# A chunked linear-attention scan with two expert layers: the order of two groups of small matmuls, and 104 rows in a third

## Chip, cores and metric

The kernel runs on one core of a Trainium2 chip. The metric is the device time of one execution in microseconds (us), as the median of several runs. The engines are called PE (TensorE), DVE (VectorE), ACT (ScalarE), POOL (GpSimd) and SP (the queue that issues most DMAs).

## What is computed

Inputs `r, k, v, w, a, b` have the shape (4 batches, 8 heads, 768 steps, 40). Each batch and head carries a 40 x 40 state through the 768 steps:

```python
for t in range(S):
    y[:, :, t] = np.einsum('bhd,bhde->bhe', rt, state)
    Sa = np.einsum('bhde,bhe->bhd', state, at)
    state_decay = state * wt[:, :, None, :] - np.einsum('bhd,bhe->bhde', Sa, bt)
    state = state_decay + np.einsum('bhd,bhe->bhde', vt, kt)
```

The output, 3072 tokens of width 320, then passes through two mixture-of-experts layers (a gate picks one of 8 experts per token; 320 to 1024, relu, back to 320, scaled by the gate's probability; the second layer adds a bias per modality to its gate). The change touches the scan alone.

## The kernel before

The 768 steps are cut into 24 chunks of 32 (`L`), four chunks to a group. Inside a chunk the recurrence is written as matrix products: a triangular system couples its 32 steps, and the state is touched once per chunk. For each chunk the methods of `Chunk` issue, in this order on PE: `x_v` (line 515) and `x_z` (522), the right side of the system from the values and from the state `zs`; `s_t(0)` and `s_t(1)` (562), transposes of the state, which ACT copies to `ssb` (563); between them `y_c` (599) of the chunk before; `r_t` (504), transposes of the next chunk's r; `u_` (533), the product with the solved triangle, whose result U is copied by ACT into `vu` next to v (537); `y_s` (589), the output's part from the state; `z_` (548), the state update; `v_t` (572), transposes of v and U, which ACT copies to `vT` (573); and `c_` (580), the products of r with v and U, masked by DVE (583). Behind `z_`, `z_up` adds the update to the state and applies the decay on DVE (554 and 556); the next chunk's `x_z` and `s_t` read the result.

The layout matters for the change. In `vu` and in the keys, the partitions 0 to 63 and 64 to 127 hold two batches (`u` = 0, 1), each as 32 steps of v (or k) and 32 rows of U (or b); the other two batches lie beside them in the free dimension (`vv` = 0, 1). In the state `zs`, partitions 0 to 63 and 64 to 127 hold heads 0 to 3 and 4 to 7 (`i2` = 0, 1; head h is 4 x `i2` + `p`), of which only the rows 0 to 39 and 64 to 103 are in use, since the head dimension is 40; the other rows are zero. So each matmul of `z_` loads 128 rows by 64 columns of keys, with a stride of 32 elements between columns, and writes to one half of the output partitions, that is, to one column half of PE's array (columns 0 to 63 or 64 to 127). `v_t` transposes 64 rows at a time, which is one row half of the array. `c_` alternates between the column halves `u` = 0 and 1 at each instruction already.

The order of the work is fixed by hand (`tc.manual_schedule`): the loop over `cc` near line 727 calls the steps one after another, and the tables `HOW`, `plan`, `todo` and `extra` put the preparation of later chunks (`aps` line 332, `kps` 345, `aab` 357), the gate of finished chunks (`xt` 1653, `lp` 1661, `rp` 974 to 976) and expert work into numbered slots between them. `Fill` spreads the solves of later triangles and decay products over DVE between the steps (lines 388, 394, 478, 481). `Warm` puts spare matmuls (`wps`, 867) ahead of some PSUM tiles, by the table `PADS`. Each engine works through its own queue in order, and PSUM tiles with the tag `tp` share three buffers.

Of the kernel before, what the change touches and what calls it, by code (L numbers as in the profile page):

```python
# [11 lines left out]
F32 = mybir.dt.float32  # L12
# [4 lines left out]
P = 128  # L17
B, H, S, D = 4, 8, 768, 40
# [36 lines left out]
def attention(tc, zones, ident, r, k, v, w, a, b, emit_x, hook0, hook1, hook2, hook3, unsafe, extra, tail):  # L55
    nc = tc.nc
    with ExitStack() as ctx:
        cp = ctx.enter_context(tc.tile_pool(name="a_const", bufs=1))
        wp = ctx.enter_context(tc.tile_pool(name="a_work", bufs=2))
        ps = Warm(tc, ctx.enter_context(tc.tile_pool(name="a_psum", bufs=1, space=PSUM)), ident)  # L60
# [431 lines left out]
        class Chunk:  # L492
# [46 lines left out]
            def z_(self):  # L539
                kb, c = self.st["kb"], self.c  # L540
                if self.cc + 1 == NCH:
                    return
                self.zps = zps = ps.tile([P, 2, 512], F32, tag="z", name="zps", bufs=1)
                for h in range(H):
                    i2, p = h // 4, h % 4
                    for vv in range(2):
                        o = zps[64 * i2 : 64 * i2 + 64, vv, 0:320].rearrange("q (u p d) -> q u p d", u=2, p=4)[:, :, p]
                        nc.tensor.matmul(out=o, lhsT=kb[:, vv, i2, :, 4 * p + c], rhs=self.vuv[:, vv, :, h, :], start=True, stop=True, skip_group_check=True)  # L548

            def z_up(self, nqlf, nc_):  # L550
                if self.cc + 1 == NCH:
# [6 lines left out]
            def s_t(self, pj):  # L558
                self.ssb = ssb = sst.rearrange("q (p b d) -> q p b d", p=4, b=4)
                sps = ps.tile([P, 4, 2, 64], F32, tag="tp", name="sps", bufs=3)  # L560
                for bb in range(4):
                    nc.tensor.transpose(out=sps[: 2 * D, bb].rearrange("q i e -> q (i e)"), in_=self.zs[:, bb, 2 * pj : 2 * pj + 2].rearrange("q p d -> q (p d)"), identity=ident)
                nc.scalar.copy(ssb[: 2 * D, pj : 4 : 2], sps[: 2 * D, :, :, 0:D].rearrange("q b i e -> q i b e"))

            def v_t(self):
                self.vT = vT = vtt.rearrange("q (u v p x) -> q u v p x", u=2, v=2, p=4)
                for u in range(2):
                    vps = ps.tile([P, 2, 4, 64], F32, tag="tp", name="vps", bufs=3)
                    s0 = slice(64 * u, 64 * u + 64)
                    for vv in range(2):  # L570
                        for hp in range(4):
                            nc.tensor.transpose(out=vps[: 2 * D, vv, hp], in_=self.vuv[s0, vv, u, 2 * hp : 2 * hp + 2].rearrange("q h d -> q (h d)"), identity=ident[s0, s0])
                    nc.scalar.copy(vT[: 2 * D, u], vps[: 2 * D])

            def c_(self):
                cps = ps.tile([P, 2, H, L], F32, tag="tp", name="cps", bufs=3)
# [74 lines left out]
        with tc.manual_schedule():  # L651
# [75 lines left out]
            for cc in range(NCH):  # L727
                g, c = cc // 4, cc % 4
# [1079 lines left out]
```

## Time and profile before

| | us |
|---|---|
| median of 3 runs | 1045.78 |
| lowest and highest | 1043.07, 1052.84 |
| the profiled execution | 1048.63 |
| its span | 1046.4 |
| PE busy in the span | 940.5 (90%) |
| DVE busy in the span | 706.4 (68%) |
| ACT busy in the span | 506.9 (48%) |

The profile is of one execution on the one core; its mean granted PE clock is 0.949 of 2.4 GHz. Each fp32 matmul appears in it as two passes, each a weight load (PEld) and a matmul (PE); a transpose appears as one. Passes overlap: the time of one includes its way through the array, so that starts lie closer together than a pass is long.

### The profile page before, as it was taken

To read this page: it belongs to the slowest core of one execution; us is meant where nothing else is said; L and a number is where in the kernel's file an instruction comes from. 1 tells how busy PE (TensorE), PEld (TensorE's weight loads), DVE (VectorE), ACT (ScalarE), POOL (GpSimd) and SP (SyncE) were. 2 spreads that over 40 slices of the span, in tenths; PEclk is the share of its full clock that TensorE was granted. 3 is DMA by queue.
4 is the path that set the end of the run, shared out by engine and by line. 5 is a ranking of instruction groups with operands and counts; after the bars stand their busy time and mean duration, and the time that the engine had idled before them with its cause. 6 is when DMAs were issued, how large, how long until landed. Compare 5 with 4: busy or idle time off the path is not lost. (4 is left out here: it accounts for less than half of the span.)

```text
span 1046.4 us, 38197 instructions
## 1 busy us (share of the span) xinstructions
PE 940.5 (90%) x16089; PEld 872.4 (83%) x16089; DVE 706.4 (68%) x2022; ACT 506.9 (48%) x991; POOL 298.5 (29%) x361
## 2 busy tenths in 40 slices
PE   7758996888897999988997989999999999999995
PEld 7747875777786888877886989999999999999995
DVE  7799868899798785863443635454556677667662
ACT  6524442443543567654441534444434456656662
POOL 6550020212111111102122425334452533233221
PEclk9769987989999999999998999999999999999998
DMA  5554423342451444234304543544534111172110
GB/s 177 135 136 110 66 82 93 63 117 62 106 125 31 104 105 99 37 52 107 80 15 111 139 130 87 143 126 115 148 88 129 38 47 46 41 233 61 36 43 26
DMA packets 152421, 96.41 MB, mean 92 GB/s; under 512 B 127407, under 2 KB 139585, under 8 KB 151850
## 3 DMA queue, kind: packets, MB, share of 16 engines
q1 hardware_dynamic: 138154, 72.53, 27.6%
q0 software_dynamic: 14080, 21.28, 7.8%
q8 instruction: 130, 2.13, 0.9%
q14 instruction: 57, 0.47, 0.2%
HBM read 112.18 MB, written 14.59 MB: 121 GB/s over the span
## 5 line engine op out<-in xcount | busy, mean ns | idle before, releaser
L1285 PE MATMUL hp<-xs,h 128*128 128x256 f32 (+1 forms) x840 | 156.1, 316 | 0.0
L1296 PE MATMUL yp<-h,hh 128*114 128x320 f32 (+1 forms) x464 | 146.6, 316 | 0.0
L1297 PE MATMUL yp<-l,hh 128*114 128x320 f32 (+1 forms) x464 | 144.1, 311 | 0.0
L1298 PE MATMUL yp<-h,hl 128*114 128x320 f32 (+1 forms) x464 | 143.9, 310 | 0.0
L1288 DVE SCALAR_TENSOR_TENSOR hl<-hp,hh 128x456 fp32r<-128x456 f32 (+1 forms) x116 | 76.6, 661 | 90.4 <-ACT hh L1287 85.2
L1285 PEld LDWEIGHTS hp<-xs,h 128*128 128x128 f32 x840 | 123.6, 189 | 3.3
L1287 ACT ACTIVATE hh<-hp 128x456 fp32r<-128x456 f32 (+1 forms) x116 | 66.5, 574 | 109.9 <-PE hp L1285 92.7
L1285 PE MATMUL hp<-xs,l 128*128 128x256 f32 (+1 forms) x504 | 101.9, 311 | 0.0
L1206 DVE TENSOR_TENSOR l<-s,h 128x768 fp32r<-128x768 f32 x88 | 80.7, 956 | 11.9 <-ACT h L1205 7.5
L1297 PEld LDWEIGHTS yp<-l,hh 128*114 128x114 f32 (+1 forms) x464 | 85.1, 183 | 0.2
L1296 PEld LDWEIGHTS yp<-h,hh 128*114 128x114 f32 (+1 forms) x464 | 85.0, 183 | 0.1
L1298 PEld LDWEIGHTS yp<-h,hl 128*114 128x114 f32 (+1 forms) x464 | 85.0, 183 | 0.0
L1285 PEld LDWEIGHTS hp<-xs,l 128*128 128x128 f32 x504 | 79.4, 188 | 3.1
L1241 POOL DMA_INDIRECT xg<-x,le x52 | 61.6, 1184 | 67.7 <-issue 50.7
L1212 DVE TENSOR_TENSOR l<-s,h 128x640 fp32r<-128x640 f32 x88 | 72.7, 826 | 3.3 <-ACT h L1211 3.3
L1353 POOL DMA_INDIRECT out<-yo,ti x28 | 33.9, 1211 | 129.7 <-ACT yo L1349 76.6
L1205 ACT CAST h<-s 128x768 fp32r<-128x768 f32 x88 | 70.4, 835 | 0.0
L1211 ACT CAST h<-s 128x640 fp32r<-128x640 f32 x88 | 63.3, 719 | 0.0
L388 DVE TENSOR_TENSOR pr<-z_sol 128x110 f32<-128x110 f32 (+20 forms) x232 | 58.1, 280 | 3.9
L977 POOL TENSOR_TENSOR ccnt<-ccnt,oh 128x8 bf16<-128x8 bf16 x24 | 5.1, 211 | 193.7 <-PE rp L975 167.8
L548 PE MATMUL zps<-vu,z_wide 128*64 128x80 f32 x512 | 56.5, 285 | 1.7 <-ACT vu L537 0.7
L995 POOL DMA_INDIRECT lst<-l2e,posi x32 | 40.0, 1250 | 61.6 <-DVE posi L988 54.3
(364 smaller groups left out, 2027.9 us busy)
## 6 DMA issues: line engine op xcount, KB each, us to landing
s<-moe_w SPq DMA_DIRECT2D x22, 1280.0 KB
s<-moe_w SPq DMA_DIRECT2D x22, 1024.0 KB
s<-moe_w SPq DMA_DIRECT2D x44, 256.0 KB
z_w<-w SPq DMA_DIRECT2D x40, 160.0 KB
z_kb<-k SPq DMA_DIRECT2D x24, 160.0 KB
z_kb<-b SPq DMA_DIRECT2D x24, 160.0 KB
z_pa<-a SPq DMA_DIRECT2D x96, 40.0 KB
rt<-r SPq DMA_DIRECT2D x96, 40.0 KB
```

The lines of the kernel that those rows point to most:

```text
L388: nc.vector.tensor_mul(prv, am[:, a:z, s : s + 1].to_broadcast([P, z - a, s + 1]), tm[:, s : s + 1, : s + 1].to_broadcast([P, z - a, s + 1]))
L1205: nc.scalar.copy(wt["h1"][:, :, s], wt["s1"][:, :, s])
L1206: nc.vector.tensor_sub(wt["l1"][:, :, s], wt["s1"][:, :, s], wt["h1"][:, :, s].bitcast(F32))
L1211: nc.scalar.copy(wt["h2"][:, s], wt["s2"][:, s])
L1212: nc.vector.tensor_sub(wt["l2"][:, s], wt["s2"][:, s], wt["h2"][:, s].bitcast(F32))
L1241: d = self.nc.gpsimd.indirect_dma_start(out=b.xg[:, h], out_offset=None, in_=b.lay.src, in_offset=IndirectOffsetOnAxis(ap=b.le[:, h, 0:1]. ...
L1285: nc.tensor.matmul(out=hp[:, i], lhsT=l, rhs=r, start=k == 0, stop=k == len(ops) - 1)
L1287: nc.scalar.activation(hh[:, s], hp, AF.Relu)
L1288: nc.vector.scalar_tensor_tensor(out=hl[:, s], in0=hp, scalar=0.0, in1=hh[:, s].bitcast(F32), op0=ALU.max, op1=ALU.subtract)
L1296: nc.tensor.matmul(out=yp, lhsT=hh[:, k, t], rhs=wt["h2"][:, k], start=k == 0, stop=False)
L1297: nc.tensor.matmul(out=yp, lhsT=hh[:, k, t], rhs=wt["l2"][:, k], start=False, stop=False)
L1298: nc.tensor.matmul(out=yp, lhsT=hl[:, k, t], rhs=wt["h2"][:, k], start=False, stop=k == 7)
```

## The change

In `z_`, the loop over heads (first all of `i2` = 0, then all of `i2` = 1) becomes a loop over `p` and `vv` with `i2` innermost, so that each instruction goes to the other column half than the one before. In `v_t`, the loop over the row halves `u` moves inside, with both `vps` tiles allocated first and the two ACT copies last. In `s_t`, the transposes read the first 104 rows of the state in place of 128, with a 104 x 104 piece of the identity as the moving matrix, and write 104 columns. The number of instructions and every product stay the same.

```diff
@@ z_
-                for h in range(H):
-                    i2, p = h // 4, h % 4
+                for p in range(4):
                     for vv in range(2):
-                        o = zps[64 * i2 : 64 * i2 + 64, vv, 0:320].rearrange("q (u p d) -> q u p d", u=2, p=4)[:, :, p]
-                        nc.tensor.matmul(out=o, lhsT=kb[:, vv, i2, :, 4 * p + c], rhs=self.vuv[:, vv, :, h, :], start=True, stop=True, skip_group_check=True)
+                        for i2 in range(2):
+                            o = zps[64 * i2 : 64 * i2 + 64, vv, 0:320].rearrange("q (u p d) -> q u p d", u=2, p=4)[:, :, p]
+                            nc.tensor.matmul(out=o, lhsT=kb[:, vv, i2, :, 4 * p + c], rhs=self.vuv[:, vv, :, 4 * i2 + p, :], start=True, stop=True, skip_group_check=True)
@@ s_t
+                n = 64 + D
                 for bb in range(4):
-                    nc.tensor.transpose(out=sps[: 2 * D, bb].rearrange("q i e -> q (i e)"), in_=self.zs[:, bb, 2 * pj : 2 * pj + 2].rearrange("q p d -> q (p d)"), identity=ident)
+                    nc.tensor.transpose(out=sps[: 2 * D, bb].rearrange("q i e -> q (i e)")[:, :n], in_=self.zs[:n, bb, 2 * pj : 2 * pj + 2].rearrange("q p d -> q (p d)"), identity=ident[:n, :n])
@@ v_t
+                vps = [ps.tile([P, 2, 4, 64], F32, tag="tp", name="vps", bufs=3) for u in range(2)]
+                for vv in range(2):
+                    for hp in range(4):
+                        for u in range(2):
+                            s0 = slice(64 * u, 64 * u + 64)
+                            nc.tensor.transpose(out=vps[u][: 2 * D, vv, hp], in_=self.vuv[s0, vv, u, 2 * hp : 2 * hp + 2].rearrange("q h d -> q (h d)"), identity=ident[s0, s0])
                 for u in range(2):
-                    vps = ps.tile([P, 2, 4, 64], F32, tag="tp", name="vps", bufs=3)
-                    s0 = slice(64 * u, 64 * u + 64)
-                    for vv in range(2):
-                        for hp in range(4):
-                            nc.tensor.transpose(out=vps[: 2 * D, vv, hp], in_=self.vuv[s0, vv, u, 2 * hp : 2 * hp + 2].rearrange("q h d -> q (h d)"), identity=ident[s0, s0])
-                    nc.scalar.copy(vT[: 2 * D, u], vps[: 2 * D])
+                    nc.scalar.copy(vT[: 2 * D, u], vps[u][: 2 * D])
```

PE's queue in chunk 15, from the last part of `aps` through `z_` and `v_t`, before (`zps` is the output of `z_`, `vps` of `v_t`, each with the number of its buffer; in brackets the queues that an instruction waits for):

```order
L332 MATMUL aps_7700<-ident_75,z_atok_72 128x128 x3
L548 MATMUL zps_7712<-vu1_147,z_wide_70 64x2x40 [waits DMAHW6_49,DMAHW5_49,Activation_49]
L548 MATMUL zps_7712<-vu1_147,z_wide_70 64x2x40 [waits DMAHW7_49,DMAHW0_49,Activation_49]
L548 MATMUL zps_7712<-vu1_147,z_wide_70 64x2x40 x14
L572 MATMUL vps_7732<-ident_75,vu1_147 80x64 [waits PE_49]
L572 MATMUL vps_7732<-ident_75,vu1_147 80x64 x7
L572 MATMUL vps_7742<-ident_75,vu1_147 80x64 [waits PE_49]
L572 MATMUL vps_7742<-ident_75,vu1_147 80x64 x7
```

and the same place after the change (the lines of `v_t` are now 573 and 575):

```order
L332 MATMUL aps_7700<-ident_75,z_atok_72 128x128 x3
L548 MATMUL zps_7712<-vu1_147,z_wide_70 64x2x40 [waits DMAHW6_49,DMAHW5_49,Activation_49]
L548 MATMUL zps_7712<-vu1_147,z_wide_70 64x2x40
L548 MATMUL zps_7712<-vu1_147,z_wide_70 64x2x40 [waits DMAHW7_49,DMAHW0_49,Activation_49]
L548 MATMUL zps_7712<-vu1_147,z_wide_70 64x2x40 x13
L573 MATMUL vps_7732<-ident_75,vu1_147 80x64 [waits PE_49]
L573 MATMUL vps_7733<-ident_75,vu1_147 80x64 [waits PE_49]
L573 MATMUL vps_7732<-ident_75,vu1_147 80x64
L573 MATMUL vps_7733<-ident_75,vu1_147 80x64
```

The first wait for the second pair of batches (`vv` = 1) moves from the second instruction of `z_` to the third, and the two `vps` buffers alternate at each of the 16 transposes, with the wait for the second one ahead of the second instruction. The rows do not show which column half an instruction of `z_` goes to; the diff does.

PE's queue in the same chunk around the state transposes (`sps`), before:

```order
L522 MATMUL xps_7419<-zs1_154,ab1_144 32x40 x32
L562 MATMUL sps_7511<-ident_75,zs1_154 80x128 [waits DVE_49]
L562 MATMUL sps_7511<-ident_75,zs1_154 80x128 x3
L599 MATMUL yps_7256<-z_wide_70,csb_7410 32x40 x32
L562 MATMUL sps_7563<-ident_75,zs1_154 80x128 [waits PE_49,Activation_49]
L562 MATMUL sps_7563<-ident_75,zs1_154 80x128 x3
```

and after:

```order
L522 MATMUL xps_7419<-zs1_154,ab1_144 32x40 x32
L563 MATMUL sps_7511<-ident_75,zs1_154 80x104 [waits DVE_49]
L563 MATMUL sps_7511<-ident_75,zs1_154 80x104 x3
L601 MATMUL yps_7256<-z_wide_70,csb_7410 32x40 x32
L563 MATMUL sps_7563<-ident_75,zs1_154 80x104 [waits PE_49,Activation_49]
L563 MATMUL sps_7563<-ident_75,zs1_154 80x104 x3
```

Nothing moves here: the same instructions stand in the same places with the same waits, and only their size differs. The queues of the other engines keep their order.

## Rows read from the trace of the kernel before

**Rows 1.** The page, busy time of each engine in the whole span.

```profile
PE 940.5 (90%) x16089; PEld 872.4 (83%) x16089; DVE 706.4 (68%) x2022; ACT 506.9 (48%) x991; POOL 298.5 (29%) x361
```

**Rows 2.** Busy us (and instructions) of PE, PEld, DVE, ACT, POOL; clock, DMA share, GB/s.

```profile
60.00:354.00 294.00, 244.95 (x7089) 214.10 (x7092) 251.32 (x844) 125.81 (x280) 46.11 (x64) 0.90 0.39 89
354.00:530.00 176.00, 161.58 (x4887) 141.36 (x4875) 112.42 (x413) 100.45 (x219) 30.50 (x49) 0.98 0.37 82
```

**Rows 3.** Waits, 60 to 354 us: us in total, times, longest.

```profile
DVE x L1646 <- PE yps L599: 7.2, 4, 4.4
DVE zs L554 <- PE zps L548: 6.3, 4, 3.3
...
DVE mx L957 <- PE lp L1661: 5.4, 2, 3.0
...
PE rp L974 <- DVE ak L362: 8.9, 1, 8.9
PE rp L974 <- DVE z_ak L362: 6.7, 4, 3.0
PE yps L589 <- DVE x L1646: 5.6, 3, 2.6
```

**Rows 4.** Waits, 354 to 530 us.

```profile
DVE zs L554 <- PE zps L548: 22.1, 7, 9.6
...
PE yps L589 <- issue: 4.5, 3, 2.7
...
PE zps L548 <- ACT vu L537: 1.0, 3, 0.5
PE yps L589 <- DVE x L1646: 0.9, 1, 0.9
```

**Rows 5.** Timeline, chunk 15: start, us, engine, line, what, [idle before <- releaser].

```profile
398.97 3.41 PE L548 MATMUL zps<-vu,z_wide 128*64 128x80 f32 x32
...
402.31 0.90 PE L572 MATMUL vps<-ident,vu 64*80 64x64 f32 x16
...
402.98 1.07 ACT L573 COPY vT<-vps 80x512 f32<-80x512 f32 x2 [1.19 <-PE vps L572]
...
404.03 0.83 DVE L556 TENSOR_TENSOR zs<-zs,qlf 128x640 f32<-128x640 f32 x1
...
404.17 1.15 PE L580 MATMUL cps<-rb,vT 128*64 128x64 f32 x32
...
407.15 0.85 PE L522 MATMUL xps<-zs,ab 128*32 128x40 f32 x46
```

**Rows 6.** Groups by shape, whole run: busy us, mean ns | idle before, releasers.

```profile
L548 PE MATMUL zps<-vu,z_wide 128*64 128x80 f32 x512 | 56.5, 285 | 1.7 <-ACT vu L537 0.7 <-issue 0.7 <-DMA rt<-r 0.3
...
L580 PE MATMUL cps<-rb,vT 128*64 128x64 f32 x768 | 28.6, 228 | 0.2 <-issue 0.2
...
L572 PE MATMUL vps<-ident,vu 64*80 64x64 f32 x384 | 23.6, 223 | 1.6 <-DVE xs__9416 L1259 0.8 <-ACT z_abd L338 0.5 <-ACT ab L338 0.2
...
L504 PE MATMUL rps<-ident,rt 128*80 128x128 f32 x96 | 14.9, 279 | 0.0
```

**Rows 7.** Windows of line 548 alone, chunk 12: PE busy (passes), clock, DMA, GB/s.

```profile
347.30:348.00 0.70, 0.70 (x9) 1.00 0.65 116
348.38:348.76 0.38, 0.38 (x10) 1.00 0.34 51
349.00:349.70 0.70, 0.70 (x9) 1.00 0.34 53
```

**Rows 8.** A window of line 580 alone, chunk 15.

```profile
404.30:405.00 0.70, 0.70 (x28) 1.00 0.56 88
```

**Rows 9.** Timeline of PE: state transposes and `r_t`, chunk 16; state transposes, chunk 12.

```profile
410.58 0.64 PE L562 MATMUL sps<-ident,zs 128*80 128x128 f32 x4
411.05 0.60 PE L504 MATMUL rps<-ident,rt 128*80 128x128 f32 x4
...
339.77 1.08 PE L562 MATMUL sps<-ident,zs 128*80 128x128 f32 x4
```

## Prediction

> **What bounds the kernel now.** I read the page first. The reader should see there that TensorE (PE) is busy for 90% of the span and VectorE (DVE) for 68% [rows 1]. All three edits lie in the scan over the 24 chunks (about 46 to 545 us); the expert layers behind it are not touched. The page's chain of waits covers only the last microseconds, so I took the scan in two stretches [rows 2]. From 60 to 354 us PE is busy 244.95 and DVE 251.32 of 294 us: neither rests much, and each waits for the other in turn. From 354 to 530 us PE is busy 161.58 of 176 us and DVE only 112.42: there PE sets the pace.
>
> The waits say the same. In the first stretch the three largest waits of DVE for PE are 7.2, 6.3 and 5.4 us, 18.9 in all, and those of PE for DVE 8.9, 6.7 and 5.6 us, 21.2 in all [rows 3]. In the second stretch DVE waits 22.1 us for the state update `zps` alone, while PE's largest wait for DVE is 0.9 us; the largest loss of PE there, 4.5 us, is "issue", time in which it waits for nothing that the profile shows [rows 4].
>
> Then the timeline of chunk 15, the steps that the change touches [rows 5]. `z_` (line 548) puts 32 passes into 3.41 us: each of its 16 matmuls appears as two, and 512 passes in the 16 chunks that take their keys from `z_wide` are 32 each [rows 6]. The transposes of v and U (line 572) take 0.90 us. ACT's two copies of `vps` start at 402.98 and take 1.07 us, and `c_` (line 580) starts at 404.17. The next `x_z` starts at 407.15.
>
> **The change, part by part.**
>
> State update, 23 times. Inside one column half the passes follow each other at (0.70 + 0.285) / 9 = 0.109 us: nine stand in a window of 0.70 us, both early and late in the step [rows 7]; the 0.285 is one pass's own length [rows 6], added since every pass that overlaps the window is counted. In the middle of the step, where the last passes of the lower half meet the first of the upper, ten stand in 0.38 us: 0.067 us each [rows 7]. So the trace of before already shows the two halves running beside each other for a few passes, with these same strided keys as weights. If all 32 alternate, a pair takes 0.109 us: 31 x 0.0545 + 0.285 = 1.97, about 2.0 us in place of 3.41. That is 1.40 us less, x 23 = 32 us of PE time.
> The bounds: `c_`, which alternates halves today with 64 moving columns and contiguous weights, has 28 passes in 0.70 us [rows 8], (0.70 + 0.228) / 28 = 0.033 us each [rows 6]; at that rate `z_` would take 1.3 us and save 2.1 us each time (49 us). On the other side, if the overlap cannot last beyond the few passes of the changeover, 31 x 0.109 + 0.285 = 3.66 us, a loss of 0.25 us each (6 us), because the present overlap in the middle goes too. I take 1.40, by the row of the same instruction.
>
> The Trainium skill speaks against this edit. "TensorE: Matmul & The Clock Gate", Part 3, "The mechanism", says that a weight load runs under matmuls in flight only where the row groups differ; both halves here use all 128 rows, so by that rule the step would stay at about 3.4 us. The trace does not agree: `c_` also uses 128 rows in both halves and runs at 0.033 us a pass.
>
> State transposes, 8 per chunk. `r_t`, the same shape, has four in 0.60 us [rows 9] with a length of 0.279 [rows 6]: (0.60 - 0.279) / 3 = 0.107 us from one to the next for 128 moving columns. With 104 columns, in proportion, 0.087: 0.02 x 8 = 0.16 us a chunk, 3.9 us in 24. Bounds: nothing (if the step has another cause), and nearly twice that at the half clock, where four take 1.08 in place of 0.64 us [rows 9]. Nothing else moves: ACT's copy reads columns 0 to 39 and 64 to 103, which are within the 104 that are kept.
>
> Transposes of v and U, 16 per chunk. The eight of the first row half are complete 0.67 us after the step begins, when ACT starts to copy them [rows 5]; if the second eight run beside them, the step ends there too, in place of 0.90 us. But ACT hides the gain: its copies still cannot start before 0.67 us, still take 1.07 us, and `c_` starts 0.12 us after the second, as it does now [rows 5]. PE reaches `c_` some 0.23 us sooner and waits there for ACT. I count nothing; the upper bound is 0.23 x 24 = 5.5 us, the lower a few hundredths of a microsecond per chunk the wrong way. Both `vps` tiles are now claimed before the first transpose; the wait for the second tile's buffer moves from the ninth instruction to the second, and the waits of these transposes for ACT's copies out of such buffers are 0.5 + 0.2 us in the whole run [rows 6]: nothing.
>
> What is late next. Behind `z_` stand `z_up` on DVE and `v_t` on PE. In chunk 15 `z_up` ends at 404.03 + 0.83 = 404.86 and `x_z` starts 2.3 us later [rows 5], so an `x_z` that comes up to that much sooner still finds the state there. `z_` itself still starts when ACT's copies of U are there (PE waits 1.0 us for them in the second stretch [rows 4]); that wait stays.
>
> The sum. Second stretch (ten state updates, eleven chunks of transposes): 10 x 1.40 + 11 x 0.16 = 15.8 us; PE is the bound, and I keep nine tenths, 14.2. First stretch (13 of each): 13 x 1.40 + 13 x 0.16 = 20.3 us of PE time; since the two engines wait for each other about equally (18.9 and 21.2 us), a microsecond taken from PE is as often on the path as off it: 10.1 us, between the 6.3 us that DVE waits for `zps` today and 20.3. Against it, the clock: the first stretch has a granted clock of 0.90 [rows 2], so 2 x 0.10 x 294 = 59 us at 1.2 GHz beside 49 us without PE work. Ten more idle us would bring some 12 us more at the lower level; work done in them takes twice as long, 6 us, half of it on the path: -3. The waits named issue, -1 (an estimate: a fifth of the 4.5 us, since PE consumes its instructions faster). Net 14.2 + 10.1 - 4 = 20.3 us. The profiled execution took 1048.63 us (span 1046.4): 1028.3. It is 2.85 us above the median of the runs, 1045.78, so for a median I expect 1025.5, rounded to 1026.
>
> **Rivals.**
> - The column halves do not overlap beyond the changeover. Only the transposes gain: 3.9 us, 1042, within 1%. For it: the weights are strided, and the overlap is seen for about ten passes only. Against it: the halves of `c_` and the changeover [rows 7, 8]. Chance 0.11. (The rule of the Trainium skill cited above would give this result.)
> - DVE keeps the first stretch: all 20.3 us of PE time there become waits for DVE, and the give-backs stay: 14.2 - 4 = 10 us, 1036. For it: DVE is busy 251 of 294 us. Against it: its 18.9 us of waits for PE. Chance 0.10, of which 0.04 falls on faster by over 1%.
> - The clock takes it back and more: slower. Place: the scan, where PE would rest longer ahead of `rp` and `y_s`, the matmuls that wait for DVE [rows 3]. Price: 0.5 us of PE time for each us at 1.2 GHz. Today that is 59 us in the first stretch and 2 x 0.02 x 176 = 7 in the second. It decides from 49 us more on the path (24.3 / 0.5); at 140 us in place of 66 the kernel would stand at 1048.6 - 24.3 + 37 = 1061 in the profile, 1058 as a median. Against it: the stretch that gains most has almost no such time (0.98). Chance 0.05.
>
> **How the numbers follow.** Forecast 1026, chance 0.74. A measurement of this kernel tells about 1% (10.5 us) from no change. Faster by over 1%: 0.74 + 0.04 = 0.78; within 1%: 0.11 + 0.06 = 0.17; slower: 0.05. The low end, 1012, is nearly all the PE time arriving (36 us would be 1010); the high end, 1040, takes in the second rival and stops short of the first.
>
> **What would show each step right or wrong.** Right: `z_` in chunk 15 at 1.9 to 2.1 us with 32 passes; four state transposes at about 0.57 us; `v_t` near 0.67 us with `c_` still 1.86 us behind its start and ACT's copies ending just before it; DVE's waits for `zps`, 6.3 + 22.1 us today, cut to under 8; chunk periods from 354 to 530 us shorter by about 1.5 us each. Wrong: `z_` at 3.4 us or more (first rival); waits of PE for DVE in the first stretch up by 15 us or more (second); a granted clock under 0.85 in the first stretch (third); or a `c_` that follows the start of `v_t` sooner than 1.7 us, which would mean that ACT did not hold it.

## The result and the profile after

The changed kernel takes 1031.74 us (median of 20 runs, 1024.36 to 1038.79), the kernel before on the same chip 1045.15 (20 runs, 1039.16 to 1054.87). The ratio is 0.987, with a 95% interval of 0.9847 to 0.9894: 13.6 us less (0.013 x 1045.15). Forecast were 1026 us and faster by over 1%; the direction is right and the range holds the result, but a third of the expected gain of 19.8 us did not arrive. The profiled execution of the changed kernel took 1031.81 us (span 1029.5), against 1048.63 (1046.4) before. Medians here and below are over all executions; a ratio is estimated without those that took over 1.5% more than the fastest of their kernel, so it need not be the quotient of the medians beside it.

First the page of the profile, busy time of each engine, to be read beside [rows 1].

```profile
PE 907.2 (88%) x16089; PEld 839.8 (82%) x16089; DVE 704.8 (68%) x2022; ACT 507.3 (49%) x991; POOL 300.6 (29%) x361
```

This row holds the whole account in short: PE is busy for 940.5 - 907.2 = 33.3 us less, with the same 16089 instructions, but the span is only 16.9 us shorter. The other 16.4 us are now time in which PE stands still. Half of the freed time arrived.

The two stretches, columns as in [rows 2].

```profile
60.00:354.00 294.00, 235.52 (x7408) 204.94 (x7410) 260.82 (x867) 132.86 (x295) 51.78 (x69) 0.88 0.41 93
354.00:530.00 176.00, 155.73 (x4772) 135.17 (x4771) 110.89 (x436) 100.02 (x221) 31.44 (x52) 0.95 0.35 77
```

In the first, PE does more instructions (7408 against 7089) in less busy time, and DVE is now busy for 260.82 of 294 us. The granted clock fell in both: 0.90 to 0.88, and 0.98 to 0.95.

The waits from 60 to 354 us, as in [rows 3].

```profile
PE rp L976 <- DVE ak L362: 10.1, 1, 10.1
PE yps L591 <- DVE x L1648: 8.4, 4, 4.1
PE rp L976 <- DVE z_ak L362: 7.9, 6, 3.7
```

These are the three rows of PE's waits for DVE that stood at 8.9, 5.6 and 6.7 us: 21.2 became 26.4. The prediction calls them the three largest, and they are not: ahead of them the view has a row that [rows 3] leaves out, the same in both kernels:

```profile
PE hv L456 <- DVE z_sol L440: 12.7, 1, 12.7
```

That wait ends at 65.9 us in the kernel before and at 65.1 in the changed one, before chunk 1. Over all rows, PE waited 38.9 us for DVE before the change and 49.5 after it. The three rows of DVE for PE went the other way, from 18.9 to 10.9:

```profile
DVE x L1648 <- PE yps L601: 5.3, 3, 3.0
...
DVE mx L959 <- PE lp L1663: 3.0, 1, 3.0
...
DVE zs L554 <- PE zps L548: 2.6, 2, 2.0
```

The waits from 354 to 530 us, as in [rows 4].

```profile
DVE zs L554 <- PE zps L548: 14.9, 4, 9.1
...
PE yps L591 <- issue: 5.6, 2, 3.8
...
PE zps L548 <- issue: 3.5, 4, 2.0
...
PE yps L601 <- issue: 2.1, 1, 2.1
PE xps L522 <- issue: 2.0, 3, 1.1
```

DVE's wait for the state update fell from 22.1 to 14.9 us. All rows of PE that are named "issue" in this stretch add up to 16.2 us, against 10.3 in the kernel before.

Chunk 15 on PE and ACT, to be read beside [rows 5].

```profile
385.19 0.70 PE L548 MATMUL zps<-vu,z_wide 128*64 128x80 f32 x8
386.15 1.63 PE L548 MATMUL zps<-vu,z_wide 128*64 128x80 f32 x24 [0.26 <-issue]
387.71 0.64 PE L573 MATMUL vps<-ident,vu 64*80 64x64 f32 x16
388.28 1.10 PE L357 MATMUL aab<-ab,kT 128*32 128x64 f32 x64
389.31 1.34 PE L582 MATMUL cps<-rb,vT 128*64 128x64 f32 x32
```

```profile
388.38 1.07 ACT L575 COPY vT<-vps 80x512 f32<-80x512 f32 x2 [0.37 <-PE vps L573]
```

`z_` is in two pieces here, with a hole named issue between them: from 385.19 to 387.78 it takes 2.59 us in place of 3.41. Chunk 14 shows it without a hole, as short as it gets; the median over the 23 updates, with holes and lower clock in it, is 2.24 us against 3.41 before:

```profile
370.41 2.07 PE L548 MATMUL zps<-vu,z_wide 128*64 128x80 f32 x32 [0.32 <-issue]
372.41 0.64 PE L573 MATMUL vps<-ident,vu 64*80 64x64 f32 x16
```

Windows inside that step, line 548 alone, as in [rows 7]: 16 and 17 passes in 0.70 us where nine stood before.

```profile
370.60:371.30 0.70, 0.70 (x16) 0.70 (x16) 1.00 0.63 103
371.50:372.20 0.70, 0.70 (x17) 0.70 (x16) 1.00 0.59 104
```

The groups by shape, as in [rows 6]: the same 512 passes of `z_` keep PE busy for 35.4 us in place of 56.5, and the 384 of `v_t` for 18.0 in place of 23.6. One pass is as long as before (289 against 285 ns): passes lie beside each other, they did not get shorter.

```profile
L548 PE MATMUL zps<-vu,z_wide 128*64 128x80 f32 x512 | 35.4, 289 | 3.5 <-issue 3.1 <-ACT vu L537 0.3
...
L573 PE MATMUL vps<-ident,vu 64*80 64x64 f32 x384 | 18.0, 229 | 3.5 <-ACT z_abd L338 1.4 <-DVE xs__9416 L1261 1.2 <-ACT ab L338 0.6
```

### The profile page after: what moved, and what is told of

Same layout as the page of the kernel before. It is cut to its first block, busy times and chain, and to the rows that moved or that the text cites. A ratio compares the mean times of both kernels' runs of the same rounds, so it can differ in the third digit from the quotient of the medians.

```text
span 1029.5 us, 38220 instructions
## 1 busy us (share of the span) xinstructions
PE 907.2 (88%) x16089; PEld 839.8 (82%) x16089; DVE 704.8 (68%) x2022; ACT 507.3 (49%) x991; POOL 300.6 (29%) x361
## 5 line engine op out<-in xcount | busy, mean ns | idle before, releaser
L1261 DVE TENSOR_TENSOR xs<-ta,xs 128x456 fp32r<-128x456 f32 (+1 forms) x28 | 18.5, 662 | 55.8 <-ACT xs L1260 55.8
```

## The experiments

All times are medians, compared with runs of the kernel before on the same chip in the same session; gains in us are (1 - ratio) x the median of the kernel before.

### One part of the change at a time

Four kernels: the new order of `z_` alone, the 104-row state transposes alone, the new order of `v_t` alone, and the first two together. Each is the kernel before with that part of the diff:

```diff
@@ z_ alone
-                for h in range(H):
+                for p in range(4):
...
+                        for i2 in range(2):
@@ s_t alone
+                n = 64 + D
...
-                    nc.tensor.transpose(out=sps[: 2 * D, bb].rearrange("q i e -> q (i e)"), in_=self.zs[:, bb, 2 * pj : 2 * pj + 2].rearrange("q p d -> q (p d)"), identity=ident)
+                    nc.tensor.transpose(out=sps[: 2 * D, bb].rearrange("q i e -> q (i e)")[:, :n], in_=self.zs[:n, bb, 2 * pj : 2 * pj + 2].rearrange("q p d -> q (p d)"), identity=ident[:n, :n])
@@ v_t alone
-                    vps = ps.tile([P, 2, 4, 64], F32, tag="tp", name="vps", bufs=3)
+                vps = [ps.tile([P, 2, 4, 64], F32, tag="tp", name="vps", bufs=3) for u in range(2)]
...
+                        for u in range(2):
```

> Only the order of the state update is changed. Theory A (the state update brings nearly all of the gain, and what is missing of the forecast is lost to later waits for instructions and to the clock): ratio to before 0.988 to 0.993, that is 7 to 13 us less; the update takes 2.1 us a chunk. Rival B (the three edits each bring a share by the PE time they free, 32, 4 and 5 us): 0.990, but then the other two alone show 1.5 and 2 us. Rival C (the update alone frees time that its neighbours take back at once): 0.997 or more.

> Only the 104 rows. Theory A: 0 to 3 us less, ratio 0.997 to 1.0; four transposes in 0.56 us. Rival B: 1.5 us, hard to tell from A. A ratio under 0.995 would say that the transposes stand on the path of every chunk.

> Only the order of the transposes of v and U. Theory A: the same time as before (ratio 0.998 to 1.002), since ACT's copies hold the next step: the transposes take 0.65 us, and the products of r with v and U still end 2.9 to 3.0 us after the transposes began. Rival B: 2 to 5 us less (0.995 to 0.998).

> The change without its edit to the transposes of v and U. Theory A: the same as the whole change, ratio 0.985 to 0.989. Rival B: 2 us slower than the whole change, 0.989 to 0.991. If the edit costs something (both buffers claimed at once), this one is faster than the whole change, under 0.985.

Measured against 1039.48 us (29 runs):

| | median us | ratio | 95% interval | us |
|---|---|---|---|---|
| z_ alone | 1028.64 | 0.9857 | 0.9816 to 0.9898 | -14.9 |
| s_t alone | 1043.21 | 1.004 | 1.0006 to 1.0074 | +4.2 |
| v_t alone | 1042.13 | 1.0027 | 0.9992 to 1.0062 | +2.8 |
| z_ and s_t | 1027.62 | 0.9849 | 0.9798 to 0.99 | -15.7 |

The state update alone brings as much as the whole change, and more than any of its three theories expected (0.988 or more). The medians, 10.8 us apart for `z_` alone and 11.9 for `z_` with `s_t`, give less than the ratios, so the sizes are good to some 4 us; the sign is not in doubt. `z_` with `s_t` cannot be told from the whole change (0.987, 0.9847 to 0.9894), so whether the edit to `v_t` costs anything isn't shown. `s_t` and `v_t` bring nothing that can be seen, although each does on PE what it says. The group of `v_t` in the kernel that has it alone: 17.5 us in place of the 23.6 of [rows 6].

```profile
L572 PE MATMUL vps<-ident,vu 64*80 64x64 f32 x384 | 17.5, 225 | 3.2 <-ACT z_abd L338 1.3 <-DVE xs__9416 L1260 1.2 <-ACT ab L338 0.6
```

That is 6 us of PE time off the engine and none off the kernel, as forecast for `v_t`; what holds it can be read in chunk 15 above (taken up in the section on the prediction). That `s_t` alone is slower by 0.4% was not forecast; its interval only just leaves out no change, and its cause is not known.

### Is every change of half needed?

The changed kernel, with `z_` in pairs: two instructions to one column half, then two to the other.

```diff
                 for p in range(4):
-                    for vv in range(2):
-                        for i2 in range(2):
+                    for i2 in range(2):
+                        for vv in range(2):
```

> The changed kernel, with the z_ matmuls in pairs: two instructions to one column half, then two to the other (8 changes of half per update in place of 15). If column halves run side by side only across a change of half, an update takes about the middle, 2.07 + 0.5 x 1.34 = 2.7 us; if a second instruction to the same half can still be taken up while the other half runs, it stays at 2.1 us. Time: 6 to 8 us more than the changed kernel in the first case, none in the second.

Measured: 1029.2 us, ratio 0.9864 (0.9835 to 0.9894), as fast as the change itself. Chunk 12 in its timeline:

```profile
341.14 2.16 PE L548 MATMUL zps<-vu,z_wide 128*64 128x80 f32 x32
```

So seven changes of half (eight pairs; the expectation counted one too many) do as well as 15, the second outcome. Two matmuls, four passes, to the same half in a row do not stop the overlap; eight matmuls, sixteen passes, as in the kernel before, do (0.109 us a pass [rows 7]). Numbers between were not tried. In pairs, `vv` changes at each instruction as it did in the kernel before, so the order of `vv` is not what brings the gain.

### Which chunks bring the gain?

The kernel before, with the new order of `z_` in a part of the chunks only: from chunk 13 on, or, in the other run, with `self.cc < 13` in the last line.

```diff
-                for h in range(H):
-                    i2, p = h // 4, h % 4
-                    for vv in range(2):
+                old = [(h, vv) for h in range(H) for vv in range(2)]
+                new = [(4 * i2 + p, vv) for p in range(4) for vv in range(2) for i2 in range(2)]
+                for h, vv in new if self.cc >= 13 else old:
```

> The kernel before, with the new order of the z_ matmuls only from chunk 13 on (10 of the 23 state updates); chunks 0 to 12 keep the old one. By the forecast's terms the late chunks alone were to bring 14.2 us on the path less 1 us of issue: 1032, ratio 0.987. Theory now (each freed microsecond of TensorE in the late chunks is given back by half in gaps of its own, for which the trace shows no other engine, and in the lower clock behind them): 6 to 7 us, ratio 0.994. Rival (the loss is all in the early chunks, where VectorE holds the end): ratio 0.987, and the early chunks alone nothing.

> The kernel before, with the new order of the z_ matmuls only in chunks 0 to 12 (13 of the 23 state updates). By the forecast's terms 10.1 us less 3 us of clock: 7 us, ratio 0.993. Theory now: 6 to 7 us, ratio 0.994, so that early and late add up to the 14.9 us of all of z_. Rival (VectorE holds the end of these chunks whatever TensorE does): within 2 us of before, ratio 0.998 or more.

Measured against 1049.56 us (11 runs): late 1040.92, ratio 0.99 (0.9863 to 0.9937), 10.5 us; early 1040.85, ratio 0.9891 (0.9849 to 0.9932), 11.4 us. Both rivals fall: the early chunks do bring something, and the late ones do not bring 0.987 by their median, though the lower end of their interval reaches it. But neither did the theory have it: each part is above the 6 to 7 us expected, and the two add up to 21.9 us, where all of `z_` brings 14.9 (by the medians 8.6 and 8.7 us, against 10.8). The intervals are some 4 us wide to each side, so whether the two gains overlap at all is not shown.

The traces give another cut. The table shows the start of `x_v` (line 515) of chunks 1, 13 and 23, and with it the two stretches between them, in eight of the profiled executions, all of kernels with every load and with all of DVE's work on DVE.

| kernel | order of `z_` | chunk 1 to 13 | chunk 13 to 23 |
|---|---|---|---|
| before | old | 263.0 | 167.2 |
| s_t alone | old | 256.3 | 171.1 |
| v_t alone | old | 258.0 | 168.0 |
| z_ early | new, then old | 256.6 | 169.0 |
| the change | new | 251.6 | 161.1 |
| z_ alone | new | 254.6 | 162.1 |
| z_ in pairs | new | 257.2 | 155.9 |
| more spare matmuls (below) | new | 258.3 | 158.3 |

The rows behind the first and fifth lines, before and after (the first start in each is `x_v` of chunk 13):

```profile
L515 PE MATMUL xps<-vd,z_ak x64: 197/197/218, 353.5 to 354.1; 32*32 32x40 f32 x64
```

```profile
L515 PE MATMUL xps<-vd,z_ak x64: 197/197/218, 341.0 to 341.6; 32*32 32x40 f32 x64
```

Without the last line, which has other work there, the first stretch has a mean of 259.1 us with the old order (three kernels) and 255.0 with the new (four); the second, with the last line, 168.8 (four) and 159.4 (four). That is 4.1 and 9.5 us, 13.6 together, and the measured gain is 13.6. In the second stretch every kernel of the new order is shorter than every one of the old; in the first the two groups overlap (251.6 to 257.2 and 256.3 to 263.0), so that the 4.1 us have a standard error of 2.4. Two further kernels of this kind are left out, since their profiled executions took 14.7 and 10.2 us more than their medians: `z_` with `s_t` (256.7 and 168.4) and `z_` late (265.3 and 164.9). With them the differences are 5.3 and 7.0 us.

The pair of before and after by itself would have told 11.4 and 6.1: the kernel before has the longest first stretch of its kind. One profile of each is not enough to say where a gain of this size lies. And the run of the early chunks alone speaks against the 4.1: its interval is 7.1 to 15.8 us. How the gain divides between the stretches is not settled.

### Are the waits named issue a matter of the transfers?

PE's longest hole in the second stretch of the changed kernel stands inside one `y_s`, in chunk 21:

```profile
475.13 0.62 PE L591 MATMUL yps<-ssb,rb 128*32 128x40 f32 x43
479.58 0.41 PE L591 MATMUL yps<-ssb,rb 128*32 128x40 f32 x21 [3.83 <-issue]
```

Windows of all engines in that hole and behind it (PE, PEld, DVE, ACT, POOL, granted clock, DMA share, GB/s):

```profile
475.80:479.50 3.70, 0.00 (x0) 0.00 (x0) 0.00 (x0) 0.76 (x2) 0.00 (x0) 1.00 1.04 227
480.40:483.70 3.30, 3.30 (x46) 2.97 (x45) 1.33 (x2) 0.31 (x1) 0.05 (x1) 0.50 1.16 273
```

But for 0.76 us of ACT, nothing but the transfer engines worked in it, and behind it the granted clock was 0.50, 1.2 GHz, for 3.3 us. So it was tried whether data transfers cause such holes. Two kernels, the kernel before and the changed one, leave out the loads of r after the first chunk and of v (both copies) after the first two.

```diff
+                if cc < 1 or (cc < 2 and x is vd):
                     for bb in range(4):
                         nc.sync.dma_start(out=x[32 * bb : 32 * bb + 32], in_=src[bb, :, t0 : t0 + L, :].rearrange("h t d -> t h d"))
...
-            for bb in range(4):
+            for bb in range(4 if cc < 2 else 0):
                 u, vv = bb % 2, bb // 2
```

> The kernel before, without the loads of r (after the first chunk) and of v (after the first two) and of v's second copy: later chunks compute with the values of the first ones, so what is left out is these transfers and nothing else. It is the base for the next run. Theory (TensorE's gaps that end on no other engine are waits for instructions, which come through the same transfer queues as the data): fewer such gaps here, 5 us or more off the time. Rival (these gaps have nothing to do with the data transfers): no more than 2 us.

> The changed kernel, with the same loads of r and v left out. Against the run with the old orders and the same loads left out: theory (what the change gives back goes to waits for instructions behind data transfers, and to the clock that falls behind them) 17 to 20 us; rival (the give-back does not come from the transfers) 12 to 15 us, as with all loads.

Measured: the kernel before without these loads 1042.04 us, ratio 0.9919 (0.9887 to 0.9952); the changed kernel without them 1028.12, 0.9767 (0.9731 to 0.9803). Between the two lie 13.9 us, as with all loads: the rival holds. The 8.5 us that the base won are not the holes either: in its trace PE's waits named issue between chunk 1 and chunk 23 add up to 23.5 us, against 24.8 in the kernel before. The second stretch of the changed kernel without the loads, first its window, then PE's largest waits:

```profile
354.00:530.00 176.00, 155.18 (x4817) 133.88 (x4804) 112.23 (x436) 100.72 (x224) 32.45 (x54) 0.98 0.15 41
```

```profile
PE xps L529 <- issue: 5.3, 5, 3.7
PE yps L608 <- issue: 4.3, 6, 2.1
```

The share of the transfer engines fell from 0.35 to 0.15, and the holes are still there. What went is PE's wait for `ak` in the first stretch ([rows 3], 8.9 us): it has no row there in the kernel before without the loads, and 1.4 us in the changed one. A row of DVE that went with it, in the kernel before, names one of these loads:

```profile
DVE z_w L206 <- DMA vu<-v: 5.9, 1, 5.9
```

So leaving out these loads does not remove the holes. What PE waits for in them can be read from the single packets in the traces. The page of the changed kernel lists a queue for instructions (packets, MB, share of 16 engines):

```profile
q8 instruction: 131, 2.15, 0.9%
```

Between the starts of `x_v` of chunk 1 and chunk 23, the fourteen traces of this case have 134 waits of PE of 0.9 us or more that are named issue. All but two of them end 1.20 to 1.65 us after a 16 KB packet of this queue has ended; such a packet comes every 4.9 us, so that a moment taken at random would stand there in 9% of the cases. And two holes of one trace that follow each other are a multiple of 256 instructions of PE apart (matmuls and weight loads, give or take one), in all 120 cases. The hole above, from 475.75 to 479.58, has one such packet in it, from 476.86 to 478.10. So PE stood there for its next block of instructions, as far as the records tell (no run changed it): the first half of the theory holds. The second half does not, since instructions have queues of their own and the holes stay without the loads. What delays a block is not shown.

### Does the lower clock cost the first stretch?

The changed kernel with 74 more spare matmuls, where its PE stood for 1.5 to 10 us.

```diff
-PADS = {..., (3, 'rp', 0): 11, (6, 'yps', 0): 1, (8, 'rp', 0): 2, (9, 'yps', 0): 2, ...}
+PADS = {..., (3, 'rp', 0): 24, (4, 'rp', 0): 12, (6, 'rp', 0): 9, (6, 'yps', 0): 15, (8, 'rp', 0): 8, (9, 'yps', 0): 12, (11, 'rp', 0): 9, (12, 'rp', 0): 6, ...}
```

> The changed kernel with more idle matmuls (wps, 128x128, results unused, 0.22 us each) ahead of eight places of chunks 3 to 12 where TensorE stands for 1.5 to 10 us in the trace of the changed kernel (rp of chunks 3, 4, 6, 8, 11, 12 and y_s of chunks 6 and 9): 74 more of them. Theory (in the first stretch the freed time is lost because TensorE's new gaps are followed by the lower clock level): time at that level from 60 to 354 us falls from 58 to under 45 us, and the kernel takes 3 to 6 us less than the changed one, 1026 to 1029. Rival (VectorE holds the end of these chunks; the clock costs nothing there): the lower level shrinks, the time stays within 2 us of the changed kernel's 1031.7, or rises by a part of the 16 us of added matmuls.

Measured: 1035.56 us, ratio 0.9904 (0.9871 to 0.9937), not faster than the change; that it is some 3 us slower isn't shown, as the two intervals overlap. Its first stretch:

```profile
60.00:354.00 294.00, 243.27 (x7400) 213.03 (x7401) 255.88 (x844) 128.87 (x287) 47.44 (x66) 0.93 0.39 90
```

```profile
PE rp L976 <- DVE z_ak L362: 7.5, 6, 2.9
PE rp L976 <- DVE ak L362: 7.0, 1, 7.0
PE yps L591 <- DVE x L1648: 2.6, 2, 2.0
```

The granted clock rose from 0.88 to 0.93 (from chunk 1 to 13, 27.3 us at 1.2 GHz in place of 58.0), and the waits for DVE shrank since spare work fills them; the stretch is not shorter (258.3). So the rival's outcome came in: the lower level shrank and the time did not. It doesn't part the two costs cleanly: the 16 us of added matmuls may have eaten what the clock gave back.

### Does VectorE hold the first stretch?

Both kernels, with the two products `kbp` x `w2` of each group moved from DVE to GpSimd (POOL).

```diff
                 for vv in range(2):
-                    nc.vector.tensor_mul(kbp[:, vv, 0 : L - 1, :], kbp[:, vv, 0 : L - 1, :], w2[:, vv, 1:L, :])
+                    nc.gpsimd.tensor_mul(kbp[:, vv, 0 : L - 1, :], kbp[:, vv, 0 : L - 1, :], w2[:, vv, 1:L, :])
```

> The changed kernel, with the two 128x1240 products kbp x w2 of each prepared group (line 224, 8 instructions, 1.41 us each on VectorE, four pairs between 117 and 319 us) given to GpSimd, which has 9 us or more before the transposes that read them. VectorE is rid of 11.3 us in the first stretch, TensorE keeps its order and its work. Theory (after the change VectorE holds most of the first stretch, so that TensorE's freed time stands there as waits for it): 5 to 9 us less than the changed kernel, 1023 to 1027, TensorE's waits for VectorE from 60 to 354 us shrink by as much. Rival (TensorE, by its lower clock and its own gaps, still sets the end): within 2 us of the changed kernel.

> The same move to GpSimd in the kernel before. Theory (there TensorE has 20 us more work in the same stretch and VectorE's relief is mostly beside it): 0 to 4 us less than before, and at least 3 us less gain than the same move brings the changed kernel. Rival (VectorE holds the first stretch in both alike): the same gain in both.

Measured against 1047.07 us (23 runs): changed kernel with the move 1041.52, ratio 0.9939 (0.9901 to 0.9977), where the change alone has 0.987; kernel before with the move 1054.53, ratio 1.0058 (1.0018 to 1.0098). The move costs 6 to 7 us in both, which neither the theory nor the rival had. The timeline of the second kernel shows what became of DVE, first DVE, then POOL:

```profile
118.34 0.34 DVE L435 TENSOR_TENSOR z_sol<-z_sol,pr 128x55 f32<-128x55 f32 x2
...
118.90 6.39 DVE L435 TENSOR_TENSOR z_sol<-z_sol,pr 128x60 f32<-128x60 f32 x2
```

```profile
119.47 5.60 POOL L224 TENSOR_TENSOR z_kb<-z_kb,z_w 128x1240 f32<-128x1240 f32 x2
```

The pair of DVE instructions just before it on the same line took 0.34 us; this one stood for 6.39 us, until POOL's two were done at 125.07. Over the first stretch the two lines of such products on DVE, L394 and L435, took 27.4 and 8.3 us in the kernel before and 35.4 and 14.3 with the move: 14 us more, where 11.0 us had been taken away. So DVE was not relieved, and the run says nothing on who holds the stretch; whether the held products make up the whole loss of 6 to 7 us isn't shown. That question is open.

## Why the prediction was right, and where its sizes were off

**The column halves.** Right. Half of the 0.109 us inside one column half, a pass was to take 0.0545 us and the step 2.0 us; (2.07 - 0.289) / 31 = 0.057, and the step takes 2.07 where no hole falls into it. The changeover of the old order [rows 7] had told that the halves overlap, not the rate: its 0.067 us a pass would have given 2.4 us. The gain is 1.34 us each, 31 us in 23 updates, against 1.40 and 32; by the medians over all updates, holes and clock included, 1.17 and 27. The first rival, 1042 us, is out: the step is far from 3.4 us, and `z_` alone brings 14.9 us. That the order of the column halves is the cause is shown twice, by `z_` alone and by the pairs. The rule of the Trainium skill ("TensorE: Matmul & The Clock Gate", Part 3, "The mechanism") that weights load under running matmuls only between different row groups does not fit this case: all passes here use the same 128 rows.

**The state transposes.** Their size is right (four take 0.55 and 0.56 us at 2.4 GHz in the changed kernel, 0.57 was forecast). That the kernel gains from it, 3.9 us by the sum, isn't shown: alone they came out 4.2 us slower, with `z_` 0.8 us faster than `z_` alone, far inside the interval.

**The transposes of v and U.** Right, and for the reason given. `v_t` takes 0.64 us, and `c_` starts 1.60 us after it and ends 2.94 us after it, against 1.86 and 3.01 before. The start looks earlier than the mark of 1.7 us that was to show ACT not holding it, but only the first instructions are: 389.31 lies before the end of ACT's second copy at 389.45, `c_` itself takes 1.34 us in place of 1.15, and its end comes 0.07 us sooner. In the trace of `v_t` alone, too, `c_` ends at a median of 3.00 us after the start of `v_t`, as was expected; there the time moves by +2.8 us with an interval that holds zero. The mark was badly set: the end of `c_`, not its start, says when ACT lets go.

**What is kept of it.** Here the sizes failed: 20.3 us were to arrive, and 13.6 did (11.1 to 16.0 by the interval). That the result still lies in the range is owed to the range's width, 28 us. Which terms were too large is read from the means over three and four profiles.

The step "PE is the bound, and I keep nine tenths, 14.2" with its 1 us for issue was to leave 13.2 us in the second stretch; the means show 9.5 (for `z_` above all, since one kernel of each group differs in `s_t`). The union of the times in which PE or its weight loads work fell from a mean of 153.2 us to 140.6 over chunks 13 to 23, so 12.5 us are off the engine; but PE's idle time there rose from 15.7 to 18.7 us, by 3.0. What rose is mostly the kind named issue, 12.0 to 14.6 us by the means (10.3 to 16.2 in the pair of before and after), where 1 us had been set aside for the whole scan. The reason given for that 1 us, PE consuming its instructions faster, fits what the holes wait for; that it is why there are more was not tested.

The step "a microsecond taken from PE is as often on the path as off it: 10.1", less 3 for the clock, was to leave 7.1 us in the first stretch; the means show 4.1. The lower clock came about as forecast (12 us more at 1.2 GHz; the means are 42 and 55 us, 13 more), but it takes some 7 us of PE time, and I had put half of that beside the path. And PE's idle time rose from 39.9 to 47.8 us, by 8.0, of which waits for DVE are 5.8 (26.6 to 32.4 by the means). So of 20.3 us some 7 went to the clock, 8 into waits, and 4 arrived, within 2 us of the whole. The half itself was read from too few rows. With every row of the view but the 12.7 us that end before chunk 1, PE waited 26.2 us for DVE and DVE 19.4 for PE; the same reasoning keeps 0.43 of 20.3, which is 8.7 us in place of 10.1 (an estimate).

That the sum was too large is shown by the measured time. This division of the loss is likely and not shown: the run of the late chunks alone has room for 13.2 as for 9.5 (6.6 to 14.4), and that of the early ones starts at 7.1, the forecast itself. That either cost, if taken away, would give its time back was tried in two ways and not shown.

**The second rival** (DVE keeps the first stretch, 1036) is right in part, by the means: four fifths of the freed time stayed there, though a third of the freed time by the clock. Its own mark, 15 us more of PE waiting for DVE, was not reached (21.2 to 26.4 in the three rows, 38.9 to 49.5 over all). **The third**, the clock, would have needed 49 us more at 1.2 GHz on the path; there were about 13 in the first stretch and 2 in the second, by the means.

**DVE's wait for the update** was to fall under 8 us from 28.4 and stands at 17.5. One wait of 9.1 us holds half of it, and it spans the hole of 3.83 us in `y_s` shown above: the state update is only the last of the things that PE does while DVE waits, so shortening it takes its own part and not the rest. The chunk periods from 13 to 23 are shorter by 0.6 us in the pair, 0.95 by the means, against 1.5.

## What to carry to other kernels

Where a matmul fills only half of the array's columns, send the instructions to the two halves in turn, at least every second one; look in the old trace for a changeover between halves, since a few passes there tell before anything is written whether the halves overlap. Of the time freed on the busiest engine half arrived here (16.9 of 33.3 us in the pair); each engine that was nearly as busy, the clock, and each wait for instructions took its part. When two engines' waits for each other are weighed, sum every row of the view and leave out those that lie outside the stretch. To say where a gain of 1% lies, profile several kernels that share the part in question, and compare the means of a stretch.

## What the runs showed of the hardware that was not expected

- A DVE product of two SBUF operands stood still beside a POOL product of two SBUF operands until that was done: 6.39 us for a pair of instructions that take 0.34 us in the kernel before, and in the next group 2.76 us for one. The means of line 435 over the first stretch show it too, the changed kernel first, then the kernel before with the move (without the move it has 203 ns for the same 50, 8.3 us):

```profile
L435 DVE TENSOR_TENSOR z_sol<-z_sol,pr 128x63 f32<-128x63 f32 (+7 forms) x47 | 7.9, 203 | 0.0
```

```profile
L435 DVE TENSOR_TENSOR z_sol<-z_sol,pr 128x60 f32<-128x60 f32 (+7 forms) x50 | 14.3, 324 | 0.0
```

  The kernel before with the move, DVE some 80 us later and once in the third group:

```profile
199.67 2.76 DVE L394 TENSOR_TENSOR z_sol<-z_sol,pr 128x31 f32<-128x31 f32 x1
...
266.17 0.49 DVE L1646 TENSOR_TENSOR x<-yps,z_gt 128x320 f32<-128x320 f32 x1 [1.12 <-PE yps L599]
```

  Such time counts as busy, so a busy DVE in the table of engines can be one that waits for POOL. The second line, a product with one operand in PSUM, was not held, although POOL's pair ran from 265.24 to 270.84. The Trainium skill states it ("SBUF — State Buffer", "SBUF: two separate sides"): the two engines take a pair of ports for a whole instruction, and against a GpSimd operation that reads SBUF a DVE operation needs it when both inputs lie in SBUF. The trace agrees.
- PE has holes of 1 to 4.6 us that wait for no other engine, many inside a run of equal matmuls, in every kernel here, 5 to 13 of them in some 420 us. They stand at multiples of 256 instructions of PE, and 132 of 134 end 1.20 to 1.65 us after a 16 KB packet of the instruction queue; which of the boundaries have one differs between executions. After the one shown the granted clock was 0.50 for 3.3 us. Taking away the loads of r and v did not remove them.
